# Gate logits with the gate's weights stationary, routing spread over the attention units, slot tables in pieces

## The chip, the cores and the metric

The kernel runs on one core of one Trainium2 chip. The metric is device time of one launch in microseconds (us), the median of several runs; lower is better. The profiled execution is one more run, taken by the hardware profiler, and its span (896.0 us) is longer than the timed median (875.09 us), so durations from it are used for differences and not as the time itself.

The engines are called as in the profile: PE is TensorE (matrix multiplications), PEld the loads of its stationary operand, DVE VectorE, ACT ScalarE, POOL GpSimd, SP the queue that issues most transfers.

## The reference

Dilated sliding-window attention over 8 sequences of 576 tokens with 8 heads of 64, followed by a mixture of 8 experts in which each token goes to its best expert. Everything is 32-bit floating point.

```python
scores = scale * np.matmul(q, k.transpose(0, 1, 3, 2))
mask_plain = (rel >= 0) & (rel < window)                       # heads 0-3, window 32
mask_dil = (rel >= 0) & (rel < window * dilation) & (rel % dilation == 0)   # heads 4-7
attn = softmax(np.where(mask, scores, -1e9))
x = (attn @ v)  # as rows: (8*576 = 4608 tokens, 512)
...
logits = x @ w_gate                       # (4608, 8)
expert_idx = np.argmax(logits, axis=1)
gate_w = softmax(logits)[np.arange(N), expert_idx]
...
for e in range(E):                        # w1 (8, 512, 1024), w2 (8, 1024, 512)
    h = np.maximum(x_sorted[lo:hi] @ w1[e], 0.0)
    y_sorted[lo:hi] = h @ w2[e]
return gate_w[:, None] * y_sorted[inv_perm]
```

## The kernel before

**Attention.** The work is cut into 32 units: 8 sequences, two kinds of heads (`ty` 0 plain, 1 dilated), two pairs of heads each (`hl`). A unit turns q and k (`turn`), computes the banded scores (`front`: 18 products of 64 x 96, on the four 64 x 64 quarters of PE's array in turn), takes the exponential on ACT, normalises on POOL (`norm`), turns the weights (`weights`) and multiplies with v (`summed`, into `xT`, the attention output with features on partitions). `weights` and `summed` of a unit come two units after its `front` (`LAG`).

**Routing.** When the four units of a sequence are through, `route(b, xT)` handles the sequence at once: it turns `xT` back into six tiles `row` of 96 tokens by 512 (L402, copied by ACT and DVE at L406), computes the logits (L413), then the best expert, the gate's weight and each token's place in its expert's bucket by a chain of some twenty small DVE instructions (L436 to L481) with two small products in between (`rank`, L455 and L462), and scatters each row tile to the DRAM tensor `bucket` with one indirect DMA from POOL (L157). In L413 a tile of `xT` (128 x 96) is the stationary operand and the 8 columns of the gate's weights `wg` move; this is done for six tiles and four blocks of features. An f32 product is carried out as two PE instructions, so these 24 products are 48 loads and 48 matmuls.

**Tables.** After sequences 1 to 7, `tables(s)` finds from the counts so far which full blocks of 128 tokens ("slots") exist, and writes for each slot its expert, its row in the bucket and whether the expert's weights have to be loaded. Each is a chain of about thirty tiny DVE instructions (L513 to L633), most on one partition. The numbers of slots that are ready after each sequence are fixed: 2, 6, 11, 15, 20, 24 and, after the last, all (39 of at most 43 exist with these inputs).

**Experts.** `moe()` handles slot after slot: load the 128 rows and the two weight matrices of 2 MB (L656, from SP), turn the rows (`xt`, L681), 32 products into `ph` (L707), ReLU to `h`, 8 products into `py` (L731), scaling (L735), an indirect DMA of the results to `out` (L740).

**The order.** All is written by one loop over three generators: each attention step yields a cost, and a planner's clock decides how many pieces of slots are put after it, and one piece of routing. After the tables of a sequence the slots that became ready are released `BEHIND` cost units later, at a rate that would finish them within `ATT` units per sequence. A scheduler of the language then fixes the order of each engine's queue, with the order of writing as priority; each engine takes its own queue in order.

**PSUM.** Every product goes to one of the 8 banks of the pool `psum` (tag `bank`), in rotation.

Of the kernel before, what the change touches and what calls it, by code (L numbers as in the profile page):

```python
# [10 lines left out]
F32 = mybir.dt.float32  # L11
# [18 lines left out]
ROW = DM + 2  # L30
# [14 lines left out]
def _constants():  # L45


    def band(j, ty):

        qi, ki = 64 * j + np.arange(64)[:, None], max(0, 64 * j - WIN) + np.arange(96)[None]  # L50
        seen = (qi - ki >= 0) & (qi - ki < WIN)
        if ty:
            seen &= qi // STRIP == ki // STRIP
        return np.where(seen, 0.0, BIG)

    def mask(ty):

        pairs = [(0, 1), (2, 3), (4, 5), (6, 7), (8, 8)]
        return np.concatenate([np.concatenate([band(j, ty) for j in two]) for two in pairs], 1)

    p = np.arange(128)
    e = np.arange(E)
    parts = {
        "mask0": mask(0),
        "mask1": mask(1),
        "ident": np.eye(128),
        "tri": np.triu(np.ones((128, 128)), 1)[:, :96],
        "ones": np.ones((128, 128)),
        "rev": np.tile(E - e, (128, 1)),
        "ecap": np.tile(e * CAP, (128, 1)),  # L70
        "tok": p[:, None] + TT * np.arange(NT)[None],
        "edge": np.tile(128 * np.arange(N // 128 + 1), (128, 1)),
        "row": p[:, None],
        "eidx": np.tile(np.minimum(np.arange(E1), E - 1), (128, 1)),
        "twice": np.tile(2 * np.arange(NSLOT), (128, 1)),
    }
    parts["first"] = np.tile(np.append(np.arange(E)[::-1] / E, -1e6), (128, 1))


    for s, (_, j0, j1) in enumerate(STAGES):  # L80
        k = np.arange(j1 - j0)
        n = (j1 - j0 + 1) // 2 if j1 < NSLOT else 0
        parts[f"list{s}"] = np.tile(k // 2 + n * (k % 2), (128, 1))
        parts[f"odd{s}"] = np.tile(k % 2, (128, 1))
    at, k, cols = {}, 0, []
    for name, a in parts.items():
        full = np.zeros((128, a.shape[1]), np.float32)
        full[: a.shape[0]] = a
        at[name] = (k, a.shape[1])
        k += a.shape[1]  # L90
        cols.append(full)
    return np.ascontiguousarray(np.concatenate(cols, 1)), at
# [3 lines left out]
def kernel(  # L96
# [17 lines left out]
    psum = ctx.enter_context(tc.tile_pool(name="psum", bufs=8, space=PSUM))  # L114
# [3 lines left out]
    wg = cpool.tile([128, 4, E], F32, name="wg")  # L118
    nc.scalar.dma_start(wg, moe_w_gate.rearrange("(c p) e -> p c e", p=128))
    counts = cpool.tile([96, E], F32, name="counts")  # L120
    nc.vector.memset(counts, 0.0)
# [201 lines left out]
    def summed(eTs, b, xT, ty, hl, part):  # L323
# [16 lines left out]
        if ty == 0:  # L340
            j0, j1 = ((0, 5), (5, 9))[part]
            for j in range(j0, j1):
                for r in range(2):
                    block(r, j, r, 64 * (j - j0))
            n = 64 * (j1 - j0)
            nc.scalar.copy(xT[:, hl, 64 * j0 : 64 * j1], xo[:, 0:n])
        else:
            for j in range(4):
                block(part, j, 0, 64 * j)
                block(part, j + 5, 1, 64 * j + 32)  # L350
            block(part, 4, 0, 256, 0, 32)
            block(part, 4, 1, 0, 32, 32)
            nc.scalar.copy(  # L353
                xT[:, 2 + hl].rearrange("p (t m a) -> p a m t", m=2, a=2)[:, part],
                xo[:, 0:288].rearrange("p (m t) -> p m t", m=2),
            )

    def attention():
# [7 lines left out]
        xTs, evs, dens = {}, {}, {}  # L366
        for i in range(len(units) + LAG):
            if i >= LAG:
                eTs = weights(evs.pop(i - LAG))
                yield 0.8, None  # L370
# [4 lines left out]
            yield 1.7, None  # L375
# [8 lines left out]
            if i >= LAG:  # L384
                b2, ty2, hl2 = units[i - LAG]
                if (ty2, hl2) == (0, 0):
                    xTs[b2] = pool.tile([128, 4, S], F32, tag="xT", name=f"xT_{b2}")
                for part in range(2):
                    summed(eTs, b2, xTs[b2], ty2, hl2, part)
                    if part == 1 and hl2 == 1 and b2 + 1 < B:  # L390
                        load_v(b2 + 1, ty2)
                    last = (ty2, hl2, part) == (1, 1, 1)
                    yield 0.9, (b2, xTs.pop(b2)) if last else None

    def route(b, xT):


        rows = []
        for i in range(NT):
            ps = bank("xrow")  # L400
            for c in range(4):
                nc.tensor.transpose(  # L402
                    ps[0:TT, 128 * c : 128 * c + 128], xT[:, c, TT * i : TT * i + TT], ident
                )
            row = pool.tile([TT, ROW], F32, tag="row", name="row", bufs=6)
            (nc.vector.tensor_copy if i % 2 else nc.scalar.copy)(row[:, 0:DM], ps[0:TT])  # L406
            rows.append(row)
            yield
        ps = bank("logits")
        lg = ps[0:TT, 0 : NT * E].rearrange("p (t e) -> p t e", e=E)  # L410
        for i in range(NT):
            for c in range(4):
                nc.tensor.matmul(  # L413
                    lg[:, i],
                    lhsT=xT[:, c, TT * i : TT * i + TT],
                    rhs=wg[:, c],
                    start=c == 0,
                    stop=c == 3,
                )
            if i == 2:  # L420
                yield
# [12 lines left out]
        top, best = small("top", NT), small("best", NT)  # L434
        oh, dl, gate = small("oh", NT, E), small("dl", NT, E), small("gate", NT)
        nc.vector.tensor_reduce(out=top, in_=lg, axis=AX, op=OP.max)  # L436
        nc.vector.tensor_tensor(out=dl, in0=lg, in1=wide(top), op=OP.subtract)

        nc.vector.tensor_scalar(oh, dl, 0.0, None, op0=OP.is_ge)
        nc.vector.tensor_tensor(out=oh, in0=oh, in1=rev, op=OP.mult)  # L440
# [6 lines left out]
        before = small("before", NT + 1, E)  # L447
        nc.vector.tensor_copy(before[:, 0], counts)
        for i in range(NT):
            nc.vector.tensor_tensor(out=before[:, i + 1], in0=before[:, i], in1=oh[:, i], op=OP.add)  # L450
        nc.vector.tensor_copy(counts, before[:, NT])
# [13 lines left out]
            rhs=before[:, 0:NT].rearrange("p t e -> p (t e)"),  # L465
# [5 lines left out]
        nc.vector.reciprocal(gate, gate)  # L471
# [10 lines left out]
        for i in range(NT):  # L482
            nc.vector.tensor_copy(rows[i][:, DM : DM + 1], gate[:, i : i + 1])
            nc.vector.tensor_scalar(
                rows[i][:, DM + 1 : ROW],
                const("tok", TT)[:, i : i + 1],
                float(b * S),
                None,
                op0=OP.add,
            )  # L490
            to_bucket(idx[:, i : i + 1], rows[i], b)
        for s, (b2, _, _) in enumerate(STAGES):
            if b2 == b:
                yield
                tables(s)
# [4 lines left out]
    def tables(s):  # L500
# [5 lines left out]
        def table(name, *dims, p=1, dt=F32):  # L506
# [3 lines left out]
        nc.tensor.matmul(tot, lhsT=const("ones", TT), rhs=counts, start=True, stop=True)  # L510
        p = 128 if last else 1
        cnt = table("cnt", E, p=p)
        nc.vector.tensor_copy(cnt, tot[0:p])  # L513

        NE = N // 128
        over, ns = table("over", E, NE, p=p), table("ns", E, p=p)
        edge = const("edge", p)[:, 0:NE] if last else const("edge", p)[:, 1 : NE + 1]
        nc.vector.tensor_tensor(
            out=over,
            in0=cnt.unsqueeze(2).broadcast_to([p, E, NE]),  # L520
            in1=edge.unsqueeze(1).broadcast_to([p, E, NE]),
            op=OP.is_gt if last else OP.is_ge,
        )
        nc.vector.tensor_reduce(out=ns, in_=over, axis=AX, op=OP.add)
# [27 lines left out]
        )  # L552
        ends, end, begin = table("ends", E1, E1), table("end", E1), table("begin", E1)
# [7 lines left out]
        nc.vector.tensor_tensor(out=begin, in0=end, in1=av, op=OP.subtract)  # L561
        place = const(f"list{s}", 1)
        if last:
# [17 lines left out]
            live.append(nc.values_load(some, min_val=SURE, max_val=NSLOT))  # L581
        shape = [1, K, E1]
# [10 lines left out]
        nc.vector.tensor_tensor(out=sel, in0=sel, in1=ge, op=OP.mult)  # L593
        ex = exs[:, j0:j1]
# [10 lines left out]
        )  # L605
        nc.vector.tensor_tensor(out=ge, in0=sel, in1=experts(first), op=OP.mult)
# [5 lines left out]
        nc.vector.tensor_scalar(base, base, float(E * CAP), None, op0=OP.min)  # L612
        if not last:
# [11 lines left out]
        if lo < j1:  # L625
# [3 lines left out]
            )  # L629
        ints = []  # L630
# [141 lines left out]
    ATT, BEHIND = 36.0, 16.0  # L772
# [32 lines left out]
    for cost, ended in attention():  # L805
# [3 lines left out]
        if ended:  # L809
            routing.append((ended[0], route(*ended)))  # L810
# [39 lines left out]
```

## Time and profile before

| | |
|---|---|
| time, median of 3 runs | 875.09 us (871.43 to 876.87) |
| span of the profiled run | 896.0 us, mean PE clock 0.948 of full |
| PE busy | 820.0 us (92% of the span) |
| PEld busy | 633.1 us (71%) |
| DVE, ACT, POOL busy | 327.4, 204.7, 143.3 us |
| moved by DMA | 187.46 MB, 209 GB/s on average |

Busy time of PE is the union of its matmuls' modelled durations. Cut by what is running, the span has five stages: up to 146.7 us attention alone; to 179 us the first slots, whose weights are being loaded; to 578 us attention and slots together; to 604 us the last routing beside slots; to 878 us nineteen slots alone, each 14.45 us. "Idle before" in a row of the profile is the time that the engine waited ahead of these instructions, with what ended the wait.

### The profile page before, as it was taken

What the parts mean: (1) busy time and instruction counts of PE and PEld (TensorE: products, weight loads), DVE (VectorE), ACT (ScalarE), POOL (GpSimd) and SP (SyncE); (2) the same over time, 40 slices, a digit from 0 to 9 for tenths busy, and PEclk for the clock granted to TensorE, in tenths of its full rate; (3) what the DMA queues carried; (4) which work ended last, traced back from release to release, by engine and by line L of the source; (5) the groups of instructions that cost most, each with busy time, mean ns of one, the idle gap of its engine ahead of it and who ended that gap; (6) DMA issues with size and microseconds to landing.
All of it is one profiled execution on the core that took longest, in us unless ns stands there. A gap on an engine that the chain in (4) does not pass through costs nothing.

```text
span 896.0 us, 18185 instructions
## 1 busy us (share of the span) xinstructions
PE 820.0 (92%) x7006; PEld 633.1 (71%) x7006; DVE 327.4 (37%) x1057; ACT 204.7 (23%) x751; POOL 143.3 (16%) x131
## 2 busy tenths in 40 slices
PE   4796978799999999999999989979999999999991
PEld 3685857677777777777777867847777676867770
DVE  4776667654643373344533441231010001101010
ACT  2562526143133222222223212100001010100000
POOL 0213132311311131113111120060000000000000
PEclk9896859889999999999999999989999999999996
DMA  9964638997999769988236546779931291549574
GB/s 196 179 149 111 132 85 305 261 249 232 326 263 309 256 180 263 293 254 284 69 118 190 189 152 228 270 233 336 322 120 48 85 308 59 209 143 322 211 250 179
DMA packets 145578, 187.46 MB, mean 209 GB/s; under 512 B 72206, under 2 KB 86030, under 8 KB 145488
## 3 DMA queue, kind: packets, MB, share of 16 engines
q1 hardware_dynamic: 137984, 165.74, 61.2%
q0 software_dynamic: 6832, 19.71, 6.3%
q8 instruction: 58, 0.95, 0.5%
q10 hardware_dynamic: 672, 0.79, 0.3%
q14 instruction: 32, 0.26, 0.1%
HBM read 216.58 MB, written 22.07 MB: 266 GB/s over the span
## 4 chain that ended last, share of the span: by engine, by line
PE 46%; issue 38%; DVE 5%; POOL 4%; DMA 2%; SPq 1%; another core or an unknown queue 1%; ACT 1%; POOLq 0%; DVEq 0%
PE ph L707 13%; PE py L731 13%; PE xo L332 4%; PE scores L269 3%; PE logits L413 3%; PE weights L317 3%; POOL out_dram L740 2%; PE xrow L402 2%; PE turned L242 2%; PE turned L234 1%; DMA k<-in_k_dram 1%; POOL bucket L157 1%; DVE e L280 1%; DMA w<-in_moe_w_dram 1%; DVE lo L289 1%
## 5 line engine op out<-in xcount | busy, mean ns | idle before, releaser
L707 PE MATMUL ph<-xt,w 128*128 128x128 f32 x2496 | 308.0, 277 | 6.3 <-issue 5.5
L707 PEld LDWEIGHTS ph<-xt,w 128*128 128x128 f32 x2496 | 293.5, 192 | 24.1 <-issue 20.9
L731 PE MATMUL py<-w,h 128*128 128x512 f32 x624 | 293.6, 608 | 6.7 <-DVE h L725 6.7
L731 PEld LDWEIGHTS py<-w,h 128*128 128x128 f32 x624 | 112.3, 193 | 112.5 <-issue 102.3
L292 ACT ACTIVATE e<-e,lo 128x96 f32<-128x96 f32 x288 | 103.6, 362 | 81.2 <-DVE lo L289 73.2
L740 POOL DMA_INDIRECT out_dram<-y,to x39 | 38.5, 986 | 401.5 <-ACT y L735 375.9
L683 DVE COPY xt<-xt 128x512 f32<-128x512 f32 x40 | 27.6, 689 | 191.9 <-PE xt L681 191.8
L307 POOL TENSOR_TENSOR e<-e,rec 128x864 f32<-128x864 f32 x32 | 52.2, 1631 | 236.7 <-DVE rec L306 147.7
L735 ACT ACTIVATE y<-py,x 128x512 f32<-128x512 f32 x39 | 26.7, 686 | 258.1 <-PE py L731 155.8
L319 DVE COPY eT<-weights 96x384 f32<-96x384 f32 x96 | 47.8, 546 | 90.1 <-PE weights L317 83.2
L725 DVE TENSOR_SCALAR h<-ph 128x512 f32<-128x512 f32 x39 | 26.9, 691 | 98.4 <-PE ph L707 86.6
L332 PEld LDWEIGHTS xo<-eT,v 96*64 96x64 f32 x1216 | 44.9, 149 | 22.4 <-issue 16.5
L157 POOL DMA_INDIRECT bucket<-row,idx x48 | 44.7, 930 | 95.1 <-DVE idx L481 31.0
L280 DVE SCALAR_TENSOR_TENSOR e<-scores,cst 128x384 f32<-128x384 f32 (+1 forms) x128 | 47.0, 399 | 27.8 <-PE scores L269 23.4
L332 PE MATMUL xo<-eT,v 96*64 96x64 f32 (+1 forms) x1216 | 52.7, 237 | 4.4 <-issue 4.4
L292 ACT ACTIVATION_READ_ACCUMULATOR e<-e,lo 128x1 f32 x288 | 53.9, 187 | 0.0
L317 PE MATMUL weights<-cst,e 128*96 128x128 f32 x288 | 44.2, 306 | 7.3 <-POOL e L307 6.4
L269 PE MATMUL scores<-kT,qT 64*64 64x96 f32 x1152 | 43.1, 284 | 8.1 <-DVE kT L239 4.5
L269 PEld LDWEIGHTS scores<-kT,qT 64*64 64x64 f32 x1152 | 35.2, 159 | 20.4 <-issue 9.9
L317 PEld LDWEIGHTS weights<-cst,e 128*96 128x96 f32 x288 | 36.7, 143 | 13.2 <-POOL e L307 8.2
L717 ACT ACTIVATE h<-ph 128x512 f32<-128x512 f32 x39 | 23.2, 596 | 97.9 <-PE ph L707 97.3
L353 ACT COPY xT<-xo 128x288 f32<-128x288 f32 x32 | 21.3, 680 | 82.0 <-PE xo L332 71.4
(103 smaller groups left out, 530.9 us busy)
## 6 DMA issues: line engine op xcount, KB each, us to landing
w<-in_moe_w_dram SPq DMA_DIRECT2D x82, 2048.0 KB
x<-bucket SPq DMA_DIRECT2D x41, 257.0 KB
v<-in_v_dram SPq DMA_DIRECT2D x32, 192.0 KB
q<-in_q_dram SPq DMA_DIRECT2D x32, 144.0 KB
k<-in_k_dram SPq DMA_DIRECT2D x32, 144.0 KB
v<-in_v_dram SPq DMA_DIRECT2D x48, 96.0 KB
q<-in_q_dram SPq DMA_DIRECT2D x8, 576.0 KB
k<-in_k_dram SPq DMA_DIRECT2D x8, 576.0 KB
```

The source lines that it names most:

```text
L157: nc.gpsimd.indirect_dma_start(out=bucket, out_offset=bass.IndirectOffsetOnAxis(ap=idx, axis=0), in_=rows, in_offset=None, bounds_check=NR ...
L269: nc.tensor.matmul(sc[r][64 * c : 64 * c + 64, 96 * (i % 5) : 96 * (i % 5) + 96], lhsT=qT[rows, 64 * j : 64 * j + 64], rhs=kT[rows, first_ ...
L280: nc.vector.scalar_tensor_tensor(out=e[p0:p1, i : i + n].rearrange("p i k -> p (i k)"), in0=sc[r][p0:p1, cols], scalar=-SCALE, in1=const(f ...
L292: nc.scalar.activation(out=e[:, n], in_=e[:, n], func=AF.Exp, bias=lo[:, n : n + 1], scale=-1.0, accum_out=den[:, n : n + 1],)
L307: nc.gpsimd.tensor_tensor(out=e, in0=e, in1=rec.unsqueeze(2).broadcast_to([128, 9, 96]), op=OP.mult)
L317: nc.tensor.transpose(tp[0:96, 128 * i : 128 * i + 128], e[:, a + i], ident)
L319: nc.vector.tensor_copy(eT, tp[0:96, 0:384])
L332: nc.tensor.matmul(xo[DH * h : DH * h + DH, at0 : at0 + nq], lhsT=vt[:, 2 * hl + r, j, :] if ty == 0 else vt[:, hl, j, DH * r : DH * r + D ...
L683: nc.vector.tensor_copy(xt, ps)
L707: nc.tensor.matmul(ph[:, fi], lhsT=w1[:, c, 128 * f : 128 * f + 128], rhs=xt[:, c], start=c == 0, stop=c == 3,)
L731: nc.tensor.matmul(py, lhsT=h[:, f], rhs=w2[:, f], start=f == 0, stop=f == 7)
L740: i = nc.gpsimd.indirect_dma_start(out=out, out_offset=bass.IndirectOffsetOnAxis(ap=to, axis=0), in_=y, in_offset=None, bounds_check=N - 1 ...
```

## The change

It has four parts.

1. **Logits.** The gate's weights become the stationary operand: `wg` is padded with zeros to 32 columns per block of features, and three products, each on its own group of 32 columns of the array (`logits[b][32*j : 32*j+32]`), stream 192 tokens each. The results lie as experts x tokens, in a PSUM bank of their own (`lpsum`; the common pool goes from 8 to 7 banks). `route` copies them to SBUF (`lgs`) and turns them with two transposes.
2. **Quarters.** `xT` holds one unit's 128 features only (three buffers). One unit later `row_part` turns that quarter of the rows (two times three transposes, one copy by ACT and one by DVE) and adds its share to the logits. The rows of a sequence are one tile of 96 x 6 x 514; the token's number is written by one POOL instruction, the gate's weight by the reciprocal itself, in place of twelve small DVE copies.
3. **Counts.** The running counts are one long tile `before` of 49 steps, which saves two copies for each sequence. In `tables` the number of full blocks comes from a shift by 7 of the integer count, in place of a comparison with 36 edges and a sum.
4. **Order.** `tables` yields seven times, so that its instructions are spread over attention steps; the steps' costs are set anew, `ATT` goes from 36 to 32 and `BEHIND` from 16 to 12.

```diff
-    psum = ctx.enter_context(tc.tile_pool(name="psum", bufs=8, space=PSUM))
+    psum = ctx.enter_context(tc.tile_pool(name="psum", bufs=7, space=PSUM))
+    lpsum = ctx.enter_context(tc.tile_pool(name="lpsum", bufs=1, space=PSUM))
...
+    wg = cpool.tile([128, 4, 32], F32, name="wg")
...
+            if i > LAG:
+                b2, ty2, hl2 = units[i - LAG - 1]
+                row_part(b2, 2 * ty2 + hl2, xT)
+                yield 0.9, b2 if (ty2, hl2) == (1, 1) else None
...
-        for i in range(NT):
-            for c in range(4):
-                nc.tensor.matmul(
-                    lg[:, i],
-                    lhsT=xT[:, c, TT * i : TT * i + TT],
-                    rhs=wg[:, c],
...
+        for i in range(0, NT, 3):
+            ps = bank("xrow")
+            for n in range(3):
+                nc.tensor.transpose(
...
+            (nc.scalar.copy, nc.vector.tensor_copy)[i // 3](
+                rows[b][:, i : i + 3, 128 * c : 128 * c + 128],
+                ps[0:TT, 0:384].rearrange("p (t d) -> p t d", t=3),
+            )
+        for j in range(3):
+            nc.tensor.matmul(
+                logits[b][32 * j : 32 * j + 32],
+                lhsT=wg[:, c],
+                rhs=xT[:, 2 * TT * j : 2 * TT * j + 2 * TT],
...
+        lgs = pool.tile([96, 2 * TT], F32, tag="lgs", name="lgs", bufs=1)
+        nc.vector.tensor_copy(lgs, logits.pop(b))
+        ps = bank("lg")
+        for i in range(2):
+            nc.tensor.transpose(
...
-        nc.vector.tensor_copy(before[:, 0], counts)
...
-        nc.vector.reciprocal(gate, gate)
+        nc.vector.reciprocal(row[:, :, DM], gate)
...
-            nc.vector.tensor_copy(rows[i][:, DM : DM + 1], gate[:, i : i + 1])
-            nc.vector.tensor_scalar(
-                rows[i][:, DM + 1 : ROW],
...
-                tables(s)
+                yield from tables(s)
...
+        nc.vector.tensor_scalar(cnti, tot[0:p], 127.0 if last else 0.0, None, op0=OP.add)
+        nc.vector.tensor_scalar(nsi, cnti, 7, None, op0=OP.logical_shift_right)
+        nc.vector.tensor_copy(ns, nsi)
...
-    ATT, BEHIND = 36.0, 16.0
+    ATT, BEHIND = 32.0, 12.0
```

More of the change, by code (lines that the diff above doesn't have):

```diff
@@ L71, in _constants @@
         "tok": p[:, None] + TT * np.arange(NT)[None],
-        "edge": np.tile(128 * np.arange(N // 128 + 1), (128, 1)),
         "row": p[:, None],
@@ L113 @@
     mpool = ctx.enter_context(tc.tile_pool(name="mpool", bufs=2))
-    psum = ctx.enter_context(tc.tile_pool(name="psum", bufs=8, space=PSUM))
+    psum = ctx.enter_context(tc.tile_pool(name="psum", bufs=7, space=PSUM))
+    lpsum = ctx.enter_context(tc.tile_pool(name="lpsum", bufs=1, space=PSUM))
     cst = cpool.tile([128, packed.shape[1]], F32, name="cst")
     nc.scalar.dma_start(cst, nc.inline_tensor(packed, name="c_pack").ap())
[L118 to L121, printed above, removed]
+    wg = cpool.tile([128, 4, 32], F32, name="wg")
+    nc.vector.memset(wg, 0.0)
+    nc.scalar.dma_start(wg[:, :, 0:E], moe_w_gate.rearrange("(c p) e -> p c e", p=128))
+    before = cpool.tile([TT, B * NT + 1, E], F32, name="before")
+    nc.vector.memset(before[:, 0], 0.0)
     blank = cpool.tile([128, ROW], F32, name="blank")
@@ L345, in summed @@
             n = 64 * (j1 - j0)
-            nc.scalar.copy(xT[:, hl, 64 * j0 : 64 * j1], xo[:, 0:n])
+            nc.scalar.copy(xT[:, 64 * j0 : 64 * j1], xo[:, 0:n])
         else:
@@ L353, in summed @@
             nc.scalar.copy(
-                xT[:, 2 + hl].rearrange("p (t m a) -> p a m t", m=2, a=2)[:, part],
+                xT.rearrange("p (t m a) -> p a m t", m=2, a=2)[:, part],
                 xo[:, 0:288].rearrange("p (m t) -> p m t", m=2),
@@ L365, in attention @@
         qT = {n: turn(0, 0, 0, n) for n in "qk"}
-        xTs, evs, dens = {}, {}, {}
-        for i in range(len(units) + LAG):
-            if i >= LAG:
+        evs, dens, xT = {}, {}, None
+        for i in range(len(units) + LAG + 1):
+            if LAG <= i < len(units) + LAG:
                 eTs = weights(evs.pop(i - LAG))
-                yield 0.8, None
+                yield 1.1, None
             if i < len(units):
@@ L374, in attention @@
                 norm(evs[i - 1], dens.pop(i - 1))
-            yield 1.7, None
+            yield 1.1, None
+            if i > LAG:
+                b2, ty2, hl2 = units[i - LAG - 1]
+                row_part(b2, 2 * ty2 + hl2, xT)
+                yield 0.9, b2 if (ty2, hl2) == (1, 1) else None
             if i + 1 < len(units):
@@ L383, in attention @@
                     load_qk(b2 + 1, ty2)
-            if i >= LAG:
+            if LAG <= i < len(units) + LAG:
                 b2, ty2, hl2 = units[i - LAG]
-                if (ty2, hl2) == (0, 0):
-                    xTs[b2] = pool.tile([128, 4, S], F32, tag="xT", name=f"xT_{b2}")
+                xT = pool.tile([128, S], F32, tag="xT", name="xT", bufs=3)
                 for part in range(2):
-                    summed(eTs, b2, xTs[b2], ty2, hl2, part)
+                    summed(eTs, b2, xT, ty2, hl2, part)
@@ L390, in attention, with row_part @@
                     if part == 1 and hl2 == 1 and b2 + 1 < B:
                         load_v(b2 + 1, ty2)
[L392 to L398, printed above, removed]
-        for i in range(NT):
+                    yield 0.75, None
+    rows, logits = {}, {}
+    def row_part(b, c, xT):
+        if c == 0:
+            rows[b] = pool.tile([TT, NT, ROW], F32, tag="rows", name=f"rows_{b}")
+            logits[b] = lpsum.tile([96, 2 * TT], F32, tag="logits", name=f"logits_{b}")
+            nc.gpsimd.tensor_scalar(
+                rows[b][:, :, DM + 1], const("tok", TT), float(b * S), None, op0=OP.add
+            )
+        for i in range(0, NT, 3):
@@ L400, in route @@
             ps = bank("xrow")
-            for c in range(4):
+            for n in range(3):
                 nc.tensor.transpose(
-                    ps[0:TT, 128 * c : 128 * c + 128], xT[:, c, TT * i : TT * i + TT], ident
-                )
[L405 to L410, printed above, removed]
@@ L411, in route @@
-        for i in range(NT):
-            for c in range(4):
-                nc.tensor.matmul(
-                    lg[:, i],
-                    lhsT=xT[:, c, TT * i : TT * i + TT],
-                    rhs=wg[:, c],
[L417 to L421, printed above, removed]
+                    ps[0:TT, 128 * n : 128 * n + 128],
+                    xT[:, TT * (i + n) : TT * (i + n) + TT],
+                    ident,
+                )
@@ new lines, in row_part, with route @@
+            (nc.scalar.copy, nc.vector.tensor_copy)[i // 3](
+                rows[b][:, i : i + 3, 128 * c : 128 * c + 128],
+                ps[0:TT, 0:384].rearrange("p (t d) -> p t d", t=3),
+            )
+        for j in range(3):
[3 more added lines that the diff above has]
+                rhs=xT[:, 2 * TT * j : 2 * TT * j + 2 * TT],
+                start=c == 0,
+                stop=c == 3,
+            )
+    def route(b):
+        row = rows.pop(b)
+        lgs = pool.tile([96, 2 * TT], F32, tag="lgs", name="lgs", bufs=1)
[3 more added lines that the diff above has]
+            nc.tensor.transpose(
+                ps[0:TT, 96 * i : 96 * i + 96], lgs[:, TT * i : TT * i + TT], ident[0:96, 0:96]
+            )
+        lg = ps[0:TT, 0:192].rearrange("p (i j e) -> p j i e", i=2, j=3)[:, :, :, 0:E]
+        yield
@@ L433, in route @@
         rev = all_tiles(const("rev", TT))
[L434 to L440, printed above, removed]
+        top, best, gate = small("top", NT), small("best", NT), small("gate", NT)
+        oh, dl = small("oh", NT, E), small("dl", NT, E)
+        nc.vector.tensor_reduce(
+            out=top.rearrange("p (j i) -> p j i", i=2), in_=lg, axis=AX, op=OP.max
+        )
+        nc.vector.tensor_tensor(
+            out=dl.rearrange("p (j i) e -> p j i e", i=2),
+            in0=lg,
+            in1=top.rearrange("p (j i) -> p j i", i=2).unsqueeze(3).broadcast_to([TT, 3, 2, E]),
+            op=OP.subtract,
+        )
+        nc.vector.scalar_tensor_tensor(
+            out=oh, in0=dl, scalar=0.0, in1=rev, op0=OP.is_ge, op1=OP.mult
+        )
         nc.vector.tensor_reduce(out=best, in_=oh, axis=AX, op=OP.max)
@@ L443, in route @@
         nc.scalar.activation(dl, dl, AF.Exp)
-        before = small("before", NT + 1, E)
-        nc.vector.tensor_copy(before[:, 0], counts)
         for i in range(NT):
-            nc.vector.tensor_tensor(out=before[:, i + 1], in0=before[:, i], in1=oh[:, i], op=OP.add)
-        nc.vector.tensor_copy(counts, before[:, NT])
+            n = b * NT + i
+            nc.vector.tensor_tensor(
+                out=before[:, n + 1], in0=before[:, n], in1=oh[:, i], op=OP.add
+            )
         yield
@@ L464, in route @@
             lhsT=const("ones", TT)[:, 0:TT],
-            rhs=before[:, 0:NT].rearrange("p t e -> p (t e)"),
+            rhs=before[:, b * NT : b * NT + NT].rearrange("p t e -> p (t e)"),
             start=False,
@@ L482, in route @@
         for i in range(NT):
-            nc.vector.tensor_copy(rows[i][:, DM : DM + 1], gate[:, i : i + 1])
-            nc.vector.tensor_scalar(
-                rows[i][:, DM + 1 : ROW],
[L486 to L491, printed above, removed]
+            to_bucket(idx[:, i : i + 1], row[:, i], b)
         for s, (b2, _, _) in enumerate(STAGES):
@@ L509, in tables @@
         tot = bank("tot")[:, 0:E]
-        nc.tensor.matmul(tot, lhsT=const("ones", TT), rhs=counts, start=True, stop=True)
+        nc.tensor.matmul(
+            tot, lhsT=const("ones", TT), rhs=before[:, (b + 1) * NT], start=True, stop=True
+        )
         p = 128 if last else 1
[L512 to L524, printed above, removed]
+        cnt, ns = table("cnt", E, p=p), table("ns", E, p=p)
+        cnti, nsi = table("cnti", E, p=p, dt=I32), table("nsi", E, p=p, dt=I32)
+        if last:
+            nc.vector.tensor_copy(cnt, tot[0:p])
+        nc.vector.tensor_scalar(cnti, tot[0:p], 127.0 if last else 0.0, None, op0=OP.add)
+        nc.vector.tensor_scalar(nsi, cnti, 7, None, op0=OP.logical_shift_right)
+        nc.vector.tensor_copy(ns, nsi)
         if last:
@@ L552, in tables @@
         )
+        yield
         ends, end, begin = table("ends", E1, E1), table("end", E1), table("begin", E1)
@@ L561, in tables @@
         nc.vector.tensor_tensor(out=begin, in0=end, in1=av, op=OP.subtract)
+        yield
         place = const(f"list{s}", 1)
@@ L581, in tables @@
             live.append(nc.values_load(some, min_val=SURE, max_val=NSLOT))
+        yield
         shape = [1, K, E1]
@@ L593, in tables @@
         nc.vector.tensor_tensor(out=sel, in0=sel, in1=ge, op=OP.mult)
+        yield
         ex = exs[:, j0:j1]
@@ L605, in tables @@
         )
+        yield
         nc.vector.tensor_tensor(out=ge, in0=sel, in1=experts(first), op=OP.mult)
@@ L612, in tables @@
         nc.vector.tensor_scalar(base, base, float(E * CAP), None, op0=OP.min)
+        yield
         if not last:
@@ L629, in tables @@
             )
+        yield
         ints = []
@@ L808 @@
         run_slots()
-        if ended:
-            routing.append((ended[0], route(*ended)))
+        if ended is not None:
+            routing.append((ended, route(ended)))
         run_routing()
```

## The prediction

> **What bounds the kernel now.** First the page, part 2, the span in 40 slices of 22.4 us: the row of PE and the clock that PE was granted.
>
> ```profile
> PE   4796978799999999999999989979999999999991
> ...
> PEclk9896859889999999999999999989999999999996
> ```
>
> From the ninth slice PE is busy to the end, but for a dent near 590 us; before that it has holes and a lowered clock. So I cut the span at the events (first slot, PE full, last routing, slots alone) and asked for busy time by stretch; the columns are the stretch, its length, busy time and count of PE, granted clock, DMA share, GB/s.
>
> ```profile
> 0.00:146.70 146.70, 108.74 (x1487) 0.81 0.67 149
> 146.70:179.00 32.30, 25.88 (x294) 0.89 1.01 304
> 179.00:578.00 399.00, 392.72 (x3538) 0.99 0.74 228
> 578.00:604.00 26.00, 19.31 (x105) 0.87 0.73 242
> 604.00:878.00 274.00, 273.38 (x1586) 1.00 0.59 204
> ```
>
> In the third and fifth stretch PE is busy 98% and over 99%: there time is PE work and nothing else. The second is bound by transfers (share 1.01): the first two slots' weights, 8 MB, go in front of a sequence's q and k. The first is bound by chains between engines, at a lowered clock.
>
> In the third stretch busy time hides what a product costs, since ends are modelled. The chain of what ended last, asked for 300 to 330 us, is there a list of PE's work with no gaps; columns are start, length, what.
>
> ```profile
> 304.18 0.73 PE xo L332 x20
> 304.91 1.09 PE ph L707 x8
> 306.00 0.44 PE xrow L402 x4
> 306.43 1.79 PE ph L707 x16
> 308.22 0.61 PE xo L332 x16
> 308.84 1.09 PE ph L707 x8
> 309.93 1.96 PE logits L413 x24
> ...
> 312.38 0.89 PE ph L707 x8
> ...
> 317.11 0.99 PE ph L707 x8
> 318.10 0.97 PE scores L269 x36
> 319.08 1.09 PE ph L707 x8
> 320.17 1.72 PE py L731 x4
> ```
>
> Read from it: `py` moves 512 columns in 1.72/4 = 0.43 us, 0.84 ns a column. A logits instruction moves 8 columns and takes 1.96/24 = 0.082 us: not the moving side but the load of 96 stationary columns sets it. A sequence has 48: 3.9 us. A transpose takes 0.44/4 = 0.11.
>
> The same rows price products on parts of the array. `xo` x16 is eight pairs of 64 columns on two column halves: 0.61 us, where sixteen one after another would take 16 x 64 x 0.84 = 0.86, so the halves work at the same time. `scores` x36 on quarters takes 0.97 against 36 x 96 x 0.84 = 2.9. But going there and back costs: `ph` x8 takes 0.89 alone, 0.99 ahead of `scores`, 1.09 after `xo` or `scores`. One visit of `xo` x16 is 0.61 + 0.20 for 8 x 64 x 0.84 = 0.43 of streaming: 0.38 over it. `scores`: 0.10 + 0.97 + 0.20 for 9 x 96 x 0.84 = 0.72: 0.55 over it.
>
> **What the Trainium skill says.** "TensorE: Matmul & The Clock Gate", Part 3: Packing small matmuls, says that products on different column groups run at the same time and gives 2.38 times for three groups of 32 columns at 512 moving columns. The trace has two halves (`xo`) and four quarters, and agrees that they overlap; three groups of 32 it doesn't have. The same page, Part 2, LDWEIGHTS, prices a load by its columns, P / 1.2 ns: an estimate of 80 ns for 96, where the trace has 82 for each logits instruction. "TensorEngine Tiling (Array Packing)", Key Properties, says that a change of tiling mode drains TensorE; the 0.38 to 0.55 us a visit agree. "PSUM — Partial Sum Buffer", Specifications, gives eight banks: the change uses all, seven of them for the common pool.
>
> **The change part by part.**
>
> *Logits.* Per quarter three products of two instructions, each of 192 columns, 0.16 us. If the three groups overlap as the halves do, the first instructions of all three go together and then the second ones: 2 x 0.16 = 0.32, plus a visit, 0.38 to 0.55; I take 0.42, 0.74 a quarter, 2.96 a sequence. Two transposes of the result add 0.22. So 3.2 against 3.9: 0.7 us less a sequence. It counts where PE is full, for sequences 3 to 7: 5 x 0.7 = 3.5, say 4 with the visit at its low end. If the groups don't overlap, a quarter is 6 x 0.16 + 0.42 = 1.38 and a sequence 5.5 + 0.2 = 5.7: 1.8 more, 9 us in all. In the first stretch the clock is 0.65 to 0.8; loads kept their 0.082 us there while streaming stretches, so I count no gain in logits at all.
>
> *Rows.* 24 transposes before and after; only their place moves. Copies: three of 682 ns on DVE and three of 577 on ACT become four each of 96 x 384 (a DVE copy of that size, `eT`, takes 546): DVE +0.1 us, plus about 0.35 for `lgs`. Gone from DVE: twelve copies of 0.14 and two of counts, 0.25 and 0.16: 2.1 us. In `tables` 0.44 + 0.43 become three of about 0.15. DVE ends some 2 us a sequence lower; in the PE-full stretch it has 168 of 399 us, so this costs and gains nothing there. The POOL instruction lies beside 237 us in which POOL waited for `rec`.
>
> *Banks.* I counted how many banks are held between first product and last copy out of them, from 200 to 570 us: never more than five. Seven are enough; cost nothing.
>
> *First stretch.* Scores of units 0 and 6 start at 12.5 and 56.0 us, 7.25 a unit; those of units 6 and 13 at 56.0 and 136.0, 11.4 a unit. These seven units carry two sequences' routing and one set of tables: 80 - 7 x 7.25 = 29 us extra. The rank products wait for DVE's chain, with everything of attention queued behind them on PE:
>
> ```profile
> 71.40 0.53 PE L455 MATMUL rank<-oh,cst 96*96 96x48 f32 x2 [2.49 <-DVE oh L442]
> ...
> 115.14 0.53 PE L455 MATMUL rank<-oh,cst 96*96 96x48 f32 x2 [3.14 <-DVE den L304]
> ```
>
> With 0.96 before L462 these are 6.6 us. The change leaves the wait (one step of attention still lies between) but shortens the chain, and puts the row work of units 0 to 6 where PE has holes. Against it, each unit gets 0.65 + 0.74 us of PE work, 14 x 1.4 = 19 us over the stretch, where before it had 24 x 0.11 + 3.9 = 6.5 a sequence, nearly the same. I take 4 us, with -3 to 12 as bounds: all of 6.6 and some of the 29 on one side, two new waits on `lgs` on the other. It moves everything after it: the last table instruction (136.7) lets the weights go (138.5), whose landing lets slot 0 start (146.7). Worked through, the planner's costs put slot 0 a third of a unit earlier and 18 slots before the end of attention, both ways; the shares of `ATT` and `BEHIND` cancel.
>
> *Tables.* In 179 to 578 PE is idle 6.3 us, most beside tables and scatters. Spreading tables may win a third: 2 us. The scatters stay.
>
> *End.* Nineteen slots alone, untouched: 274 us. Slots 20 to 23 are ready long before the last tables, so a shorter last routing gains nothing.
>
> Sum: 4 + 4 + 2 = 10 us, 875 - 10 = 865.
>
> **The rivals.**
>
> *The groups don't overlap.* For it: no three groups of 32 in this trace. Against: both forms that use parts of the array overlap. +9 where PE is full, +3 in the first stretch for longer streams at the lowered clock, -2 for tables: 885. This is the slower side.
>
> *New waits eat it.* PE now waits in 32 places for ACT's copies of `xT` (at L402 it waited 2.4 us for eight sequences) and eight times for `lgs`. If each of the 18 quarters where PE is full costs 0.3 and each `lgs` 1 us: 5 + 5 = 10 against the gain of 10, and a unit's delay of the first tables 1: 876. Against it: slot pieces stand between.
>
> *The first stretch gains much more.* If tables no longer run after their place in the order (they ended at 136.7, when unit 13 began, though written with unit 11), 14 us come from there: 4 + 14 + 2 = 20: 855.
>
> **Chances.** Forecast 0.50, no overlap 0.14, new waits 0.18, the larger gain 0.18. The bound for faster is 866. The forecast's spread is about 8 us to either side: 0.33 of it below 866, 0.17 within 1%. The larger gain adds 0.17, new waits 0.03 to faster and 0.13 to same, no overlap 0.03 to same. Faster 0.53, same 0.33, slower 0.14. The range 850 to 882 cuts the worse half of no overlap and the better third of the larger gain.
>
> **What would show it.** Right: logits instructions of three start within some 20 ns, about 0.16 us for the three; a quarter with its visit near 0.74; `ph` after it longer by 0.2; the last table instruction of sequence 1 near 132 instead of 136.7; the stretch between full PE and end of attention shorter by about 6; 14.45 us a slot as before. Wrong: logits starting 0.16 apart; PE waits on `lgs`, `xT` or `xrow` in rows with more than 5 us in sum; slot 0 waiting for its weights.

## The result, and the profile after

The changed kernel takes 849.67 us (846.35 to 854.23, four runs) against 875.98 us (871.43 to 881.16, four runs) before: a ratio of 0.970, 95% interval 0.963 to 0.978. A later set of six runs gave 849.32 us, ratio 0.969 (0.966 to 0.972). That is 26 us less, where 10 were forecast, and just outside the range of 850 to 882.

The first profile of the kernel before, from which the prediction was made, was of an execution with 20 us of stalls that its timed runs don't have (a span of 896 us beside 876); a second one has 874.0, and all differences below are taken from that second one. The page of the changed kernel, PE and its clock in 40 slices, now of 21.1 us:

```profile
span 845.4 us, 17772 instructions
...
PE   3778779999898999999999999999999999999991
...
PEclk9798799999999999999999999999999999999996
```

PE is full from the seventh slice but for two at 8 tenths, and the dent near 590 us is gone. To see which stretch gave the time, both kernels are cut at the same four events: the start of slot 0's first product, the end of slot 1's last, the start of slot 19, the end of the last slot. First the kernel before (second profile), then the changed one; the columns are as in the prediction.

```profile
0.00:140.10 140.10, 105.25 (x1488) 0.82 0.70 158
140.10:212.50 72.40, 65.23 (x653) 0.86 0.88 251
212.50:565.50 353.00, 351.68 (x3185) 1.00 0.74 234
565.50:855.40 289.90, 289.82 (x1688) 1.00 0.61 214
```

```profile
0.00:126.80 126.80, 92.36 (x1407) 0.87 0.77 178
126.80:186.70 59.90, 58.07 (x643) 0.97 1.01 278
186.70:537.00 350.30, 344.96 (x3099) 1.00 0.76 238
537.00:826.70 289.70, 289.70 (x1687) 1.00 0.61 215
```

The slots alone are as before. The first two rows are 13.3 and 12.5 us shorter, the third 2.7. But the cut is not quite fair: at the end of slot 1 the scores of 19 units had begun before and of 18 now, so the third row holds one unit more. An estimate of what a unit is worth: 17 slots of 14.45 us are 246 of the 345 us that PE is busy in the changed kernel's third row, which leaves 99 us for 14 units, 7 each. So about 19 us come from ahead of the end of slot 1, and nearly 10 from the stretch in which PE is full. Together that is the 28.6 us by which these two profiles differ; the timed medians differ by 26.

The logits are what was expected of them in kind. PE's instructions of one quarter in the full stretch, in order of time (start, length with the modelled end, line, count):

```profile
254.30 1.05 PE L735 MATMUL ph<-xt,w 128*128 128x128 f32 x8
255.19 0.82 PE L414 MATMUL xrow<-cst,xT 128*96 128x128 f32 x6
255.94 0.53 PE L424 MATMUL logits<-xT,wg 128*32 128x192 f32 x6
256.39 2.05 PE L735 MATMUL ph<-xt,w 128*128 128x128 f32 x16
258.28 0.67 PE L245 MATMUL turned<-cst,q 72*128 72x72 f32 x8
```

The three instructions of a group start 7 ns apart, as was forecast for groups that overlap. Read by starts: six logits instructions of 192 columns take 256.39 - 255.94 = 0.45 us. One after another they would take 6 x 0.16 = 0.97; three at a time twice is 0.32. `xrow` x6 takes 0.75 where six times 0.11 is 0.66, so 0.09 goes to entering; `ph` x16 takes 1.89 where 0.112 each is 1.79, so 0.10 to leaving. A quarter is 0.64 us.

### The profile page after: what moved, and what is told of

It reads as the page before. It is cut to its first block, busy times and chain, and to the rows that moved or that the text cites. A ratio compares the mean times of both kernels' runs of the same rounds, so it can differ in the third digit from the quotient of the medians.

```text
span 845.4 us, 17772 instructions
## 1 busy us (share of the span) xinstructions
PE 785.1 (93%) x6830; PEld 590.7 (70%) x6830; DVE 317.5 (38%) x955; ACT 203.3 (24%) x759; POOL 145.4 (17%) x139
## 4 chain that ended last, share of the span: by engine, by line
PE 48%; issue 30%; DVE 7%; DMA 5%; ACT 3%; POOL 2%; SPq 2%; POOLq 0%; DVEq 0%; ACTq 0%
PE py L759 16%; PE ph L735 15%; PE xo L335 4%; PE weights L320 3%; DMA x<-bucket 3%; PE scores L272 3%; ACT e L295 2%; POOL out_dram L768 2%; PE xrow L414 2%; PE turned L237 1%; PE turned L245 1%; DVE lo L292 1%; PE logits L424 1%; DVE e L283 1%; DMA k<-in_k_dram 1%
## 5 line engine op out<-in xcount | busy, mean ns | idle before, releaser
L735 PE MATMUL ph<-xt,w 128*128 128x128 f32 x2496 | 304.9, 277 | 2.9 <-DVE xt L711 2.9
L759 PE MATMUL py<-w,h 128*128 128x512 f32 x624 | 288.5, 600 | 0.5 <-DVE eT L322 0.5
L310 POOL TENSOR_TENSOR e<-e,rec 128x864 f32<-128x864 f32 x32 | 52.1, 1629 | 205.3 <-DVE rec L309 118.1
L335 PEld LDWEIGHTS xo<-eT,v 96*64 96x64 f32 x1216 | 42.4, 144 | 18.7 <-issue 10.4
L160 POOL DMA_INDIRECT bucket<-rows,idx x48 | 44.7, 932 | 37.0 <-DVE idx L513 17.5
L335 PE MATMUL xo<-eT,v 96*64 96x64 f32 (+1 forms) x1216 | 49.4, 232 | 0.0
L320 PE MATMUL weights<-cst,e 128*96 128x128 f32 x288 | 41.4, 293 | 3.8 <-POOL e L310 3.8
L320 PEld LDWEIGHTS weights<-cst,e 128*96 128x96 f32 x288 | 34.1, 135 | 10.5 <-issue 4.9
L272 PEld LDWEIGHTS scores<-kT,qT 64*64 64x64 f32 x1152 | 31.1, 148 | 12.7 <-issue 5.8
L272 PE MATMUL scores<-kT,qT 64*64 64x96 f32 x1152 | 37.6, 268 | 2.4 <-DVE kT L242 2.3
L356 ACT COPY xT<-xo 128x288 f32<-128x288 f32 x32 | 21.1, 678 | 63.7 <-PE xo L335 63.6
```

Source lines behind the costliest of these rows:

```text
L160: nc.gpsimd.indirect_dma_start(out=bucket, out_offset=bass.IndirectOffsetOnAxis(ap=idx, axis=0), in_=rows, in_offset=None, bounds_check=NR ...
L272: nc.tensor.matmul(sc[r][64 * c : 64 * c + 64, 96 * (i % 5) : 96 * (i % 5) + 96], lhsT=qT[rows, 64 * j : 64 * j + 64], rhs=kT[rows, first_ ...
L310: nc.gpsimd.tensor_tensor(out=e, in0=e, in1=rec.unsqueeze(2).broadcast_to([128, 9, 96]), op=OP.mult)
L320: nc.tensor.transpose(tp[0:96, 128 * i : 128 * i + 128], e[:, a + i], ident)
L335: nc.tensor.matmul(xo[DH * h : DH * h + DH, at0 : at0 + nq], lhsT=vt[:, 2 * hl + r, j, :] if ty == 0 else vt[:, hl, j, DH * r : DH * r + D ...
L735: nc.tensor.matmul(ph[:, fi], lhsT=w1[:, c, 128 * f : 128 * f + 128], rhs=xt[:, c], start=c == 0, stop=c == 3,)
```

## The experiments

Three theories were set against each other. **A**: the gain is PE work taken out where PE is full. **B**: it is made in the first stretch, by routing that ends sooner; later **B2**, that the quarters do this. **C**: it is the cheaper logits plus tables in pieces, wherever the rows are turned. One set of four kernels met a level of 900 us for the kernel before instead of 876, so those are compared by their ratio to it. Each set of experiments ran on another chip, this one on the chip that the record calls 5; whether the chip makes the level was not shown. One kernel was timed in both kinds of set and has nearly the same ratio, 0.976 and 0.978; the changed kernel was not run in the set at 900.

**The kernel before again.**

> The kernel before, unchanged, for a second profile. The first profile of it has a span of 896 us beside a timed median of 876, the profile of the changed kernel 845 beside 850, so the two profiles differ by 51 us where the times differ by 26. If the 20 us too many are a matter of that one execution, the stall of PE at 590 us (6.9 us of waiting and 3.5 us at half clock) and DVE's 6 us of waiting at 121 us should be gone and the span be near 876; if they belong to the kernel, both come back at the same places.

Measured: 875.73 us, span 874.0. The stall at 590 us is gone: from slot 19's first product to slot 20's are 15.1 us in place of 24.6. The first tables end at 129.5 in place of 136.7. The 20 us belonged to that execution.

**Part 1 alone.** In the kernel before, the logits at the end of a sequence in the new form:

```diff
-                    lhsT=xT[:, c, TT * i : TT * i + TT],
-                    rhs=wg[:, c],
...
+                    lhsT=wg[:, c],
+                    rhs=xT[:, c, 2 * TT * j : 2 * TT * j + 2 * TT],
```

> The kernel before with part 1 alone: the gate's weights stationary on three column groups, computed at the end of the sequence as before, eight banks in one pool, rows, tables and planner as before. Theory A (the gain is PE work taken out where PE is full): 1.4 us a sequence for five sequences and something ahead of them, 866 to 869 us. Theory B (the gain is made in the first stretch, by routing that is spread over the units and ends sooner): 872 to 878, since the first tables come no sooner.

Measured: 856.23 us, ratio 0.978 (0.975 to 0.981). That is 19 us, more than either theory allowed. Cut at the same events:

```profile
0.00:134.60 134.60, 96.19 (x1444) 0.82 0.71 167
134.60:200.80 66.20, 60.69 (x632) 0.92 0.97 269
200.80:543.10 342.30, 340.12 (x3073) 1.00 0.76 241
```

Here both kernels have begun 19 units at the second cut, so the rows compare directly: 5.5 + 6.2 = 11.7 us ahead of the end of slot 1 and 10.7 after it. The groups of PE's logits matmuls, of the kernel before (second profile) and of this one (count, busy us, mean ns, idle before):

```profile
L413 PE MATMUL logits<-wg,xT 128*96 128x8 f32 x384 | 37.4, 236 | 0.0
```

```profile
L413 PE MATMUL logits<-xT,wg 128*32 128x192 f32 x192 | 12.0, 329 | 0.0
```

25 us of PE's time go, and 2.8 come back in the transposes `lg`. Split by the cuts, logits are busy 16.1 us ahead of the end of slot 1 before and 4.5 here; less 1.1 us that `lg` costs there, 10.5 of the 11.7 us. The gain is busy time and not waiting: over the first two rows PE's busy time falls by 13.6 us, and its idle time grows by 1.9. The 3.1 us of busy time that logits and `lg` don't account for go with a higher granted clock in the second row (0.92 in place of 0.86); whether the clock is cause or consequence was not separated. After the cut logits and `lg` together fall by 11.9 us, beside the 10.7 measured. The first tables end at 122.5 us in place of 129.5, although theory B expected them no sooner.

Why the old logits cost 5.4 us a sequence ahead of the cut and 4.2 after it shows in the third sequence of the kernel before. The granted clock is 1.00 during the first of these rows and 0.50 during the second:

```profile
148.10 2.21 PE L413 MATMUL logits<-wg,xT 128*96 128x8 f32 x24
...
152.57 3.90 PE L413 MATMUL logits<-wg,xT 128*96 128x8 f32 x24
156.33 2.06 PE L707 MATMUL ph<-xt,w 128*128 128x128 f32 x8
```

The second half takes 156.33 - 152.57 = 3.76 us where the first takes 2.06. From start to start that is 85 ns for one instruction and 160 ns. So the loads of 96 columns do slow with the clock.

**Part 1 undone.** In the changed kernel each quarter of `xT` is stationary again, and DVE sums four partial logits:

```diff
-                lhsT=wg[:, c],
-                rhs=xT[:, 2 * TT * j : 2 * TT * j + 2 * TT],
...
+                lhsT=xT[:, TT * i : TT * i + TT],
+                rhs=wg[:, c, 0:E],
```

> The changed kernel with part 1 undone: each quarter of xT is stationary again and the gate's 8 columns move, 48 instructions a sequence as before; the four quarters' logits are summed by one DVE reduction in place of the copy and the two transposes. Quarters, tables in pieces and planner stay. Theory A: 7 to 10 us of the 26 go, 857 to 860 us. Theory B: 850 to 854, and the first tables still end near 112 us.

Measured: 858.47 us, ratio 0.980 (0.977 to 0.983): 9 us of the 26 are lost. That is A's number, but not in A's place. Cut at the same events, with 18 units begun at the second cut as in the changed kernel:

```profile
0.00:135.80 135.80, 105.95 (x1468) 0.89 0.72 172
135.80:197.90 62.10, 59.90 (x665) 0.97 1.02 262
197.90:550.30 352.40, 350.47 (x3191) 1.00 0.74 236
```

Beside the rows of the changed kernel the first two are 9.0 and 2.2 us longer, and the third only 2.1, although PE is busy 5.5 us more in it: with the new logits PE idles 5.3 us there in place of 1.9, most of it waiting for a slot's rows. The first tables end at 120.6, where B had them near 112. So most of the loss lies ahead of the end of slot 1, as B's gain did, but it comes from PE's work, as A's did.

The rest of the change is worth 17 us beside the old logits, but only 7 beside the new ones (856 to 849). In time the two parts share 10 us. In the end of the first tables they hardly share: 129.5 before, 122.5 with part 1 alone, 120.6 with the rest alone, 112.3 to 114.1 with both.

**Tables in one piece** in the changed kernel:

```diff
-                yield from tables(s)
+                for _ in tables(s):
+                    pass
```

> The changed kernel with its tables written in one piece again. Theory A: no difference, 848 to 852 us. Theory B, if it is the pieces that let the tables end sooner or keep them out of attention's way on DVE: 855 to 862; if it is the quarters, no difference either, with the first tables ending near 112 us or sooner.

Measured: 857.54 us, ratio 0.981 (0.976 to 0.985): 8 us slower, yet the first tables end at 113.0, as with the pieces (112.3). So it isn't the tables' end. PE's order shows what it is; first this kernel, then the changed one:

```profile
118.45 0.78 PE L335 MATMUL xo<-eT,v 96*64 96x64 f32 x20
125.12 2.05 PE L736 MATMUL ph<-xt,w 128*128 128x128 f32 x8 [5.89 <-DMA w<-in_moe_w_dram]
```

```profile
119.74 1.04 PE L272 MATMUL scores<-kT,qT 64*64 64x96 f32 x36
...
126.77 1.26 PE L735 MATMUL ph<-xt,w 128*128 128x128 f32 x8 [2.95 <-DVE xt L711]
```

Seven fewer steps of routing release slot 0 sooner by the planner's clock. PE comes to it about a unit earlier in its order and waits 5.9 us for weights whose load is issued no sooner (115.7 us, 115.0 in the changed kernel); unit 13's scores, which start at 119.7 in the changed kernel, stand behind it and start at 131.9. Later PE also waits for a slot's rows from `bucket`:

```profile
243.47 1.09 PE L710 MATMUL xt<-cst,x 128*128 128x128 f32 x4 [7.79 <-DMA x<-bucket]
```

The changed kernel has such waits of 2.3 and 2.3 us in one profile and of 3.1 in the other. So the pieces act through the planner here, which puts slots in PE's order ahead of what they need. How much of the 8 us is each wait was not separated.

**Tables in pieces alone** (in the set at 900 us): the seven `yield` lines in the kernel before.

> The kernel before with its tables in pieces and nothing else. Theory C: 866 to 870 us, 6 to 9 less. Theory B2 (pieces matter only beside the quarters and their planner): 873 to 878.

Measured: ratio 1.006 (1.003 to 1.008), a little slower. By themselves they bring nothing; C falls in this form.

**The planner's constants.** 36 and 16 in the changed kernel (in the set at 900), 32 and 12 in the kernel before and beside part 1 alone, 28 and 8 in the changed kernel:

```diff
-    ATT, BEHIND = 32.0, 12.0
+    ATT, BEHIND = 28.0, 8.0
```

> The changed kernel with the planner's ATT and BEHIND back at 36 and 16. If the constants carry a part of the gain (slots earlier in the order), 853 to 858 us, with slot 0 starting some 5 us later; if they only fit the order to the new steps, 848 to 852.

> The kernel before with ATT 32 and BEHIND 12 and nothing else. If the constants alone are worth 1 to 2 per cent (as the two kernels with 36 and 16 against their siblings suggest): a ratio of 0.980 to 0.990. If they help only where routing ends sooner: 0.995 to 1.005, with slot 0 waiting for its weights.

> Part 1 alone (ratio 0.978) with ATT 32 and BEHIND 12. If the constants work by themselves, 0.963 to 0.970, level with the changed kernel or better; if they need the quarters and the pieces, 0.976 to 0.982.

> The changed kernel with ATT 28 and BEHIND 8. If bringing slots earlier goes on paying, 0.96 to 0.966; if 12 is the point where slot 0 just meets its weights, 0.970 to 0.985, with PE waiting for w at slot 0.

Measured, as ratios: 0.989 (0.984 to 0.995), 1.004 (1.002 to 1.006), 0.978 (0.974 to 0.982) and 0.976 (0.972 to 0.980). Going back to 36 and 16 costs the changed kernel 2 per cent, by ratios of two sets. In their own sets the new constants help neither the kernel before nor part 1 alone, and going on to 28 and 8 loses 6 us against 32 and 12. In the kernel before with 32 and 12, PE again meets slot 0 ahead of its weights:

```profile
139.96 2.05 PE L707 MATMUL ph<-xt,w 128*128 128x128 f32 x8 [4.22 <-DMA w<-in_moe_w_dram]
```

With part 1 the same wait is 5.3 us, with 28 and 8 it is 2.2 us. The longest waits for a slot's rows are 3.4, 3.5 and 5.3 us in these three, and there is none above 0.2 us in the kernel before or in part 1 alone with 36 and 16. So pieces and constants seem to set one thing together, the place of the slots in PE's order against the landing of their weights and rows: in the changed kernel each without the other loses. The changed kernel with both taken back, tables in one piece and 36 and 16, was not run.

**Without quarters.** `xT` by sequence, rows turned and all logits made at its end, attention steps as before; part 1, the rows' one tile, counts and pieces stay. With 36 and 16, and with 32 and 12 (both in the set at 900), then with 32 and 12 again at the usual level:

> The changed kernel without quarters: xT by sequence, rows turned and all twelve logits products made at the end of the sequence in one visit, attention steps, ATT and BEHIND as before; kept are the stationary weights, the rows in one tile, the counts and the tables in pieces. Theory B2 (quarters spread the routing and are a good part of the gain): 855 to 860 us, no better than part 1 alone with 856. Theory C (the gain is cheaper logits plus tables in pieces, wherever the rows are turned): 847 to 851, since the pieces bring what undoing them cost, 8 us, and a single visit is 0.9 us a sequence cheaper than four.

> The kernel without quarters, with ATT 32 and BEHIND 12 as in the changed kernel. If earlier slots are worth something with the whole-sequence routing too: 3 to 5 us below its sibling with 36 and 16; otherwise equal within 2 us, or slower where slot 0 then waits for its weights.

> The kernel without quarters with ATT 32 and BEHIND 12 once more, because its first set had another level of the kernel before (900 us). If quarters are worth something beside cheaper logits, pieces and constants: a ratio of 0.975 to 0.985, against 0.969 of the changed kernel. If they are worth nothing: 0.966 to 0.972.

Measured: 0.983 (0.980 to 0.987), 0.976 (0.972 to 0.979), and in the last 857.28 us, 0.978 (0.974 to 0.981). The first two, from one set, are 886.10 and 877.56 us: here the new constants are worth 8.5 us, more than the 3 to 5 expected. The last is no better than part 1 alone (0.978) and 8 us behind the changed kernel (849.32 in a set at the same level). So the quarters bring that 8 beside the rest, and counts, pieces and constants together bring nothing without them: as to the time, B2 holds for this part. With one visit a sequence these logits are even cheaper on PE (0.9 us, the expectation said), so the quarters win more elsewhere than they lose. In the profile the first tables end at 117.9 in place of 112.3 to 114.1, and after slot 0's start PE waits once for a sequence's q, queued behind the weights:

```profile
141.75 0.53 PE L415 MATMUL logits<-xT,wg 128*32 128x192 f32 x6
149.43 1.19 PE L237 MATMUL turned<-cst,q 96*128 96x96 f32 x6 [7.15 <-DMA q<-in_q_dram]
```

The changed kernel has no such wait above 1 us. In the same profile slot 20 takes 18.5 us in place of 14.5. How much of the 8 us each of these three is was not separated.

**The new waits.** The rows of PE's idle time in the changed kernel name `lgs` and `xT`, which the second rival had feared. One kernel puts an attention step between `lgs` and its transposes, the other writes a quarter's rows after the next unit's turns:

```diff
         nc.vector.tensor_copy(lgs, logits.pop(b))
+        yield
         ps = bank("lg")
```

> The changed kernel with one attention step between the copy lgs and the two transposes that read it. PE waited 1.3 to 2.3 us for lgs in each of the first three sequences. If these waits lie on the path: 2 to 5 us less, a ratio of 0.963 to 0.967, with no wait on lgs above 0.5 us. If they only take the place of other waits of the first stretch, or routing that ends a step later costs as much: 0.968 to 0.974.

> The changed kernel with a quarter's rows and logits written after the turns of the next unit instead of ahead of them, so that ACT's copy of xT is over by then (PE waited 1.1 to 1.8 us for it three times ahead of L414). If that wait lies on the path: 0.963 to 0.967. If the place of the row work doesn't matter: 0.967 to 0.972; if routing that ends two steps later delays the first tables: 0.972 to 0.980.

Measured: 852.83 us, 0.973 (0.969 to 0.977), and 859.55 us, 0.980 (0.976 to 0.984). With the step in between, PE's waits for `lgs` in the first two sequences shrink from 2.3 and 1.5 us to 1.4 and 0.8; with the rows after the turns two of the three waits for `xT` are gone. But others came: for `xT` of 3.3 and 2.3 us close to slot 0's start, and in the second kernel for `lgs` of 3.1 and 2.3 us and one of 7.7 us for a slot's rows. The first tables end at 118.1 and 118.6 in place of 114.1, and slot 0 starts 7 us later (135.2 and 136.1 in place of 128.6). By slot 1's end 19 units have begun here and 18 in the changed kernel, so a part of that is order. That an earlier end of routing is worth more than these waits fits both results, but the second kernel's new wait for rows is a rival that was not tested. No kernel tried was faster than the changed one.

## Why the prediction was wrong

*The direction and the mechanism of the logits were right.* Three column groups overlap, the first rival (no overlap) is out. Where PE is full, a quarter took 0.64 us where 0.74 was worked out, a visit 0.32 where 0.42 was taken from `xo` and `scores`. A sequence then costs 2.8 with its transposes in place of 3.2, against 3.9, which is 1.1 us less for five sequences: 5.5 in place of 4. With the old logits put back PE is busy 5.5 us more there, but only 2.1 us of it show in the time, since PE waits less. The rest of that stretch's 10 us was not traced to a part. This is a small miss of one term.

*The step that failed is the term "First stretch", 4 us, and with it the sentence on the logits, "so I count no gain in logits at all".* About 19 us came from ahead of the end of slot 1. The sentence rested on "loads kept their 0.082 us there while streaming stretches". Three of the four pieces of logits ahead of slot 0 were at full clock in the profile before. In the fourth, 14 instructions ran at a granted clock of 0.50:

```profile
107.54 2.30 PE L413 MATMUL logits<-wg,xT 128*96 128x8 f32 x14
109.77 2.24 PE L269 MATMUL scores<-kT,qT 64*64 64x96 f32 x36
```

From their start to the next group's these 14 take 2.23 us, 0.16 each, twice the 0.082. Part 1 alone took 11.7 us out of the time ahead of the end of slot 1, and logits with `lg` 10.5 us of PE's busy time there. The prediction called the first stretch bound by chains, and PE does idle 34.8 of its 140.1 us. Still, 6.3 us less of logits ahead of slot 0 brought its start 5.5 us forward and the end of the first tables 7.0. What fits is that routing's chain and the attention around it share PE's one order of work, in which 48 logits instructions stood ahead of both; PE's work there was on the path nearly in full.

*The rest of that term.* With the quarters the row work no longer stands at the end of a sequence, and they are worth another 8 us beside the new logits; by which way is open. The granted clock ahead of the end of slot 1 is higher as well (0.87 and 0.97 in the changed kernel's first two rows, 0.82 and 0.86 before), which no run tells apart from the rest. The third rival's mechanism, "tables no longer run after their place in the order", was seen: they ended at 112.3 to 114.1 in place of 129.5. But it isn't the quarters' alone, since part 1 alone brought them to 122.5. The rival was given 0.18, and its 855 us are still 5 above what was measured.

*"Spreading tables may win a third: 2 us" is not borne out.* In pieces alone the kernel before came out 0.6% slower; in the changed kernel one piece lost 8 us, by the order of the slots and not by shorter tables. *"The shares of `ATT` and `BEHIND` cancel"* is right for the kernel before (1.004) and part 1 alone (no change), and wrong without quarters (8.5 us) and, by ratios of two sets, in the changed kernel. *"DVE ends some 2 us a sequence lower"*: its busy time fell by 7.2 us in all, 0.9 a sequence; no cost or gain of it was seen.

*The second rival's waits came.* The page of waits has 4.6 us ahead of `lg` and 6.3 ahead of `xrow`, 10.9 together and above the "more than 5 us in sum" that the prediction named as a sign against it. They were outweighed; taking them away the two ways tried made the kernel slower. *Banks and the end* were as said: 14.45 us a slot, and no wait for a bank stands out.

## What to carry to other kernels

A product with few moving columns cost the load of its stationary side here (0.082 us for 96 columns, with 8 moving): put the small operand there, and let idle column groups take the rest of the tokens; from start to start a sequence's logits took 1.43 us of PE in one visit and 4 x 0.45 in four. A stretch in which PE is 75% busy at a lowered clock can still be paced by PE's work, where the chain and the work around it share one order on PE; price removed work there at the clock it really ran at, not at zero. A planner's release point is right when the consumers meet their data: after any change that moves either side, read the waits of the first slots for weights and for rows. PE waited 2 to 6 us for the first weights in four of the slower kernels here, and over 5 us once for rows in three.

## What the runs showed of the hardware that was not expected

Visits to parts of the array differ in price: three groups of 32 columns cost about 0.32 us over streaming, the quarters of `scores` 0.55. All twelve products of a sequence in one visit took 1.43 us from their first start to the next group's, where the streaming alone is 8 x 0.16 = 1.29:

```profile
380.54 1.50 PE L413 MATMUL logits<-xT,wg 128*32 128x192 f32 x24
381.97 1.13 PE L745 MATMUL py<-w,h 128*128 128x512 f32 x2
```

In the set at 900 us, and in the first profile of the kernel before, PE shows pauses of about 1 to 2 us ended by nothing that the profile names. The densest group lies beside the last scatters into `bucket` (with tables in pieces alone, six between 576 and 587 us). After slot 0's start they sum to 13 to 17 us in the four profiles of that set, to 6 us in that first profile, and to at most 1.5 us in all others. Their cause was not traced.
